# The sign of a 64-bit weight's upper word from GpSimd, one VectorE step fewer per weight block, and every step in a new order

## The chip, the cores and the metric

The kernel runs on one core of a Trainium2 chip. The metric is the device time of one execution in microseconds (us). TensorE (PE, with its weight loads as PEld), VectorE (DVE), ScalarE (ACT), GpSimd (POOL) and the DMA queue of SyncE (SP) each work through their own instructions in order, and semaphores hold an instruction until what it needs is there.

## What is computed

Batch 8, 8 heads, 576 tokens, head size 64, in single precision. Attention keeps only scores within `tau` of the row's maximum; what it gives is the input of a gated MLP that mixes tokens.

```python
scores = scale * np.matmul(q, k.transpose(0, 1, 3, 2))
thresh = np.max(scores, axis=-1, keepdims=True) - tau
scores = np.where(scores >= thresh, scores, -1000000000.0)
attn = softmax(scores)                      # exp, divided by the sum
x = (attn @ v) laid out as (batch, 576, 512)
h = gelu(x @ w_in)                          # 512 -> 1024, tanh form
u, v = h[..., :512], h[..., 512:]
v_n = (v - mean(v)) / sqrt(var(v) + 1e-06) * g_ln
v_s = einsum('ts,bsd->btd', w_sg, v_n) + b_sg
out = x + (u * v_s) @ w_out
```

`w_in` and `w_out` come to the kernel as 64-bit floats, seen as pairs of 32-bit words, and are turned on the chip into a single-precision number and its remainder. `out` is stored transposed.

## The kernel before

A first pass writes down a plan of 4646 steps (`at(kind, key, fn)`, without running them); then `issue` runs them in the sequence of the list `ORDER`, written out by hand as numbers of steps. So `ORDER` sets the order on every engine and queue. `PLACES` gives for each use of PSUM which of the 8 banks it takes.

Attention goes over 32 units `n` of two heads. A unit loads q, k and v, scales q (`q_scale`, L522), copies the last 64 tokens into a tile (`q_tails`, L527), and then goes over five blocks of query tokens: `scores` (L546; L553 for the last block) into two PSUM banks, `maxima` on DVE (L562), `threshold` on POOL (L566), `select` on ACT (L576), `exponentials` on ACT (L582), `turn_blocks` on DVE (L630). The turned blocks go through DRAM and back (`put_blocks`, `get_blocks`), `values` multiplies them by v (L661), `scale_rows` on DVE (L669, L671) divides by the sums, and `x_hi`, `x_lo`, `x_tail` (L676, L679, L682) split the result. Four units make a batch, and `moe(b)` needs all four: products L753, for the first units of batch 0 in two parts (L769, `in_two`), joined on DVE (L779); gelu on ACT and DVE (L725, L738, L740, L732), statistics (L839, L842) on DVE, normalisation on POOL and ACT (L846 to L874), output L961 and a store L964.

The weights are prepared while the first units run. `from_double` runs for 12 blocks of 128x512 numbers (eight of `w_in`, jobs 0 to 7, and four of `w_out`, jobs 14 to 17): `w_load` (L385) brings the words; `magnitude` (L393, ACT) takes the upper word's size times 2^16; `word` step 0 (L398, POOL) bounds it; step 1 (L400, DVE) shifts left by 4 and right by 1, which moves the exponent and leaves the sign bit empty; step 2 (L402, DVE) takes the upper word's sign bit and joins it; step 3 (L404, DVE) keeps sign and exponent; `w_mul` (L413, DVE) multiplies by the lower word; then the high part and the rest, on POOL (L418, L431, L433) or by PE (L424) and ACT (L429). `from_single` does the same for `w_sg` (L460, L461), `tail_weights` (L473, L474) and `bias` for its end. Sixteen `warm` matmuls (L988) of a constant fill gaps on PE.

```python
            elif step == 1:
                engine.tensor_scalar(bits, bits, 4, 1, ALU.logical_shift_left, ALU.logical_shift_right)
            elif step == 2:
                engine.scalar_tensor_tensor(bits, t["up"], 0x80000000, bits, ALU.bitwise_and, ALU.bitwise_xor)
```

Of the kernel before, what the change touches and what calls it, by code (L numbers as in the profile page):

```python
# [12 lines left out]
F32 = mybir.dt.float32  # L13
F32R = mybir.dt.float32r
U32 = mybir.dt.uint32
# [227 lines left out]
def tile_threshold_attention_gated_mlp(  # L243
# [133 lines left out]
    def from_double(src, home, early, put, k):  # L377
# [9 lines left out]
        def magnitude():  # L387
            if early:
                both = cpool.tile([P, 2 * FH], F32, tag=f"z{k % NM}", name=f"wz{k}")
                t["full"], t["pow"] = both[:, 0:FH], both[:, FH:2 * FH]  # L390
            else:
                t["full"], t["pow"] = spares(sp, FH)
# [656 lines left out]
```

## Time and profile before

| | us |
|---|---|
| median of 3 runs | 869.17 (864.87 to 869.45) |
| the profiled execution | 875.15 |
| its span, first to last instruction | 873.3 |
| PE busy | 822.1 (94%) |
| DVE, ACT, POOL busy | 640.5 (73%), 637.8 (73%), 459.9 (53%) |
| granted TensorE clock, mean | 0.978 of full speed |

The profile's page cuts the span into 40 slices. The shares of busy time are means over stages with different limits, so each stage has to be read by itself: the windows view gives busy times by stretch, the waits view who waited for whom, the timeline the instructions in order. A busy PE is not PE at its peak: at half clock the same matmul is busy twice as long.

### The profile page before, as it was taken

Reading aid. Unit: us, or ns where it says so; the run is one execution under the profiler, and the core shown is the slowest. Engines: PE = TensorE matmul, PEld = TensorE weight load, DVE = VectorE, ACT = ScalarE, POOL = GpSimd, SP = SyncE. Lnnn points to the kernel's source line nnn. Section 1 sums busy time; section 2 is a strip of 40 time slices with the busy share of each in tenths; the row PEclk is TensorE's granted clock in tenths of the full one; section 3 lists DMA queues with packets and bytes.
Section 4 is the critical chain, followed back from the end, with each engine's and each line's share of the span. In section 5 each row is a group of like instructions: output and inputs, shape, how many; then the busy total and the mean of one; then the engine's idle time right before and its main releaser. Section 6 shows DMA issues by size and latency. Waiting matters only on the chain.

```text
span 873.3 us, 24720 instructions
## 1 busy us (share of the span) xinstructions
PE 822.1 (94%) x9726; PEld 668.9 (77%) x9726; DVE 640.5 (73%) x1142; ACT 637.8 (73%) x1346; POOL 459.9 (53%) x785
## 2 busy tenths in 40 slices
PE   6788889999999899999999999999999999999998
PEld 3456667876888778887788878887678878887898
DVE  6999798865978477873878848786787838786264
ACT  6868578756988577885779768886697849787271
POOL 3576387443754457443564348534564357535283
PEclk9799999998999999999999999999999999999999
DMA  8897942794676935777356964688466962777401
GB/s 311 205 256 223 259 126 69 208 243 105 180 194 179 222 95 144 199 195 203 109 160 178 230 179 116 168 236 233 131 152 165 250 173 69 183 220 202 108 8 62
DMA packets 218998, 151.74 MB, mean 174 GB/s; under 512 B 32257, under 2 KB 204289, under 8 KB 218882
## 3 DMA queue, kind: packets, MB, share of 16 engines
q1 hardware_dynamic: 218882, 150.16, 64.7%
q8 instruction: 76, 1.25, 0.6%
q14 instruction: 40, 0.33, 0.1%
HBM read 97.68 MB, written 52.43 MB: 172 GB/s over the span
## 4 chain that ended last, share of the span: by engine, by line
PE 53%; DMA 14%; POOL 9%; DVE 8%; ACT 6%; issue 5%; SPq 5%; POOLq 0%; DVEq 0%; ACTq 0%
PE all_banks L753 32%; PE all_banks L546 10%; PE all_banks L661 8%; DMA ir<-ird 4%; DMA pt<-swb 4%; DMA ird<-ir 3%; PE all_banks L553 2%; DVE columns L562 2%; ACT p L576 2%; DMA swb<-pt 2%; SPq L647 2%; ACT p L582 2%; POOL x L679 1%; POOL ot L961 1%; POOL vv L861 1%
## 5 line engine op out<-in xcount | busy, mean ns | idle before, releaser
L576 ACT ACTIVATE p<-all_banks,columns 128x576 f32<-128x576 f32 x288 | 201.7, 737 | 79.2 <-POOL columns L566 78.1
L562 DVE TENSOR_REDUCE columns<-all_banks 128x1 f32<-128x576 f32 x288 | 205.4, 745 | 73.2 <-PE all_banks L546 62.5
L582 ACT ACTIVATE p<-p,columns 128x576 f32<-128x576 f32 x288 | 221.1, 772 | 0.8
L630 DVE STREAM_TRANSPOSE pt<-p 128x576 f32<-128x576 f32 x288 | 208.3, 753 | 16.7 <-ACT p L582 12.1
L546 PE MATMUL all_banks<-rk,rq 64*64 64x288 f32 x2048 | 167.6, 425 | 8.2 <-POOL rq L522 3.3
L661 PE MATMUL all_banks<-pt,rv 64*64 64x128 f32 (+1 forms) x4608 | 156.4, 286 | 14.1 <-DMA pt<-swb 10.7
L661 PEld LDWEIGHTS all_banks<-pt,rv 64*64 64x64 f32 x4608 | 145.1, 134 | 26.0 <-DMA pt<-swb 8.0
L566 POOL TENSOR_TENSOR columns<-columns 128x2 f32<-128x2 f32 (+1 forms) x160 | 35.8, 224 | 207.5 <-DVE columns L562 190.3
L546 PEld LDWEIGHTS all_banks<-rk,rq 64*64 64x64 f32 x2048 | 78.1, 136 | 62.2 <-issue 16.0
L753 PE MATMUL all_banks<-wsh,z 128*128 128x288 f32 (+2 forms) x512 | 116.1, 307 | 2.3 <-ACT p L576 1.9
L753 PE MATMUL all_banks<-wi,x 128*128 128x512 f32 x424 | 113.4, 406 | 5.1 <-ACT p L576 2.5
L753 PE MATMUL all_banks<-x,wi 128*128 128x288 f32 (+2 forms) x720 | 114.9, 301 | 0.1
L753 PEld LDWEIGHTS all_banks<-x,wi 128*128 128x128 f32 x720 | 100.8, 188 | 13.5 <-issue 5.9
L753 PE MATMUL all_banks<-gh,wo 128*128 128x288 f32 (+1 forms) x480 | 107.4, 300 | 0.7 <-DVE ir L671 0.7
L961 POOL TENSOR_TENSOR ot<-ot,x 128x288 f32<-128x288 f32 x112 | 89.9, 808 | 21.6 <-ACT ot L970 19.4
L753 PEld LDWEIGHTS all_banks<-wi,x 128*128 128x128 f32 x424 | 75.9, 189 | 26.8 <-issue 4.0
L753 PEld LDWEIGHTS all_banks<-wsh,z 128*128 128x128 f32 x512 | 85.4, 191 | 14.1 <-issue 5.8
L753 PEld LDWEIGHTS all_banks<-gh,wo 128*128 128x128 f32 x480 | 79.7, 188 | 10.7 <-issue 3.4
L753 PE MATMUL all_banks<-wsl,z 128*128 128x288 f32 (+2 forms) x256 | 74.9, 300 | 0.0
L679 POOL TENSOR_TENSOR x<-ir,x 128x576 fp32r<-128x576 f32 x32 | 45.6, 1425 | 52.8 <-ACT x L676 52.3
L753 PE MATMUL all_banks<-gl,wo 128*128 128x288 f32 (+1 forms) x240 | 70.4, 298 | 0.4 <-POOL gl L936 0.4
L669 DVE TENSOR_TENSOR ir<-all_banks,ir 128x512 f32<-128x512 f32 x32 | 21.9, 684 | 57.3 <-PE all_banks L661 31.8
(161 smaller groups left out, 1147.0 us busy)
## 6 DMA issues: line engine op xcount, KB each, us to landing
rv<-in_vP SPq DMA_DIRECT2D x32, 576.0 KB, 5.3
swb<-pt SPq DMA_DIRECT2D x64, 180.0 KB, 3.7
swb<-pt SPq DMA_DIRECT2D x32, 360.0 KB, 3.9
pt<-swb SPq DMA_DIRECT2D x64, 180.0 KB, 4.7
pt<-swb SPq DMA_DIRECT2D x32, 360.0 KB, 5.3
rq<-in_qT SPq DMA_DIRECT2D x32, 288.0 KB, 4.4
rk<-in_kT SPq DMA_DIRECT2D x32, 288.0 KB, 4.2
swa<-pt SPq DMA_DIRECT2D x32, 288.0 KB, 4.0
```

Of the source, the lines that this page charges most:

```text
L546: nc.tensor.matmul(st["s", h, i][cols, a, 0:HALF], st["q"][rows, i * P + c * D:i * P + (c + 1) * D], st["k"][rows, a * HALF:(a + 1) * HALF ...
L553: nc.tensor.matmul(sc[:, a, 0:HALF], tails[part], st["k"][:, a * HALF:(a + 1) * HALF], start=True, stop=True)
L562: return lambda: nc.vector.tensor_reduce(nm, st["s", h, i][:, :, 0:HALF], AX.XY, ALU.max, negate=True)
L566: return lambda: nc.gpsimd.tensor_tensor(nt, nm, toff[:, 0:1] if i == NM else toff, ALU.subtract)
L576: nc.scalar.activation(halves(st["p", h, i]), st["s", h, i][:, :, 0:HALF], AF.Prelu, bias=columns_of(i)[1][:, h:h + 1], alpha=BIG)
L582: return lambda: nc.scalar.activation(st["p", h, i], st["p", h, i], AF.Exp, bias=toff[:, 0:1], accum_out=l_of[part][:, c:c + 1])
L630: nc.vector.transpose(out, st["p", h, i].rearrange("p (j x) -> p j x", x=BLK))
L661: nc.tensor.matmul(st["acc"][h * D:(h + 1) * D, r, :, c0:c0 + w], v[rows, c, h], x[:, :, h * w:(h + 1) * w], start=(c == 0), stop=(c == PA ...
L669: nc.vector.tensor_tensor(main, acc[:, :, 0:MAINQ], main, ALU.mult)
L679: nc.gpsimd.tensor_tensor(xl_of[b, hp], st["ir"], xh_of[b, hp], ALU.subtract)
L753: nc.tensor.matmul(st["acc"][0:rows[0]] if rows else st["acc"], w, x, start=(j == 0), stop=(j == n - 1))
L961: return lambda: nc.gpsimd.tensor_tensor(o(), o(), x[b, m][:, ts_], ALU.add)
```

## The change

Three things change. The steps of a weight block: step 1 moves from DVE to POOL and becomes the upper word, read as a float, times 0.0 (times 1.0), written to the tile `pow`: zero with the word's sign. Step 2 stays on DVE, now shifts the bounded size left by 3 and joins the sign in the same instruction, from `bits` and `pow`. So a block has three DVE steps instead of four, and two POOL steps of 128x512 instead of one. A function `places` allocates the tiles `full` and `pow` at whichever of the steps comes first, since the sign needs only the loaded words. `ORDER` is new as a whole (4646 steps, the same numbers with the same meanings), and so is `PLACES` (the same 580 uses).

```diff
+        def places():
+            if "full" in t:
+                return
...
         def word(step, engine):
+            places()
             bits = t["full"].bitcast(U32)
...
             elif step == 1:
-                engine.tensor_scalar(bits, bits, 4, 1, ALU.logical_shift_left, ALU.logical_shift_right)
+                engine.tensor_scalar(t["pow"], t["up"].bitcast(F32), 0.0, 1.0, ALU.mult, ALU.mult)
             elif step == 2:
-                engine.scalar_tensor_tensor(bits, t["up"], 0x80000000, bits, ALU.bitwise_and, ALU.bitwise_xor)
+                engine.scalar_tensor_tensor(bits, bits, 3, t["pow"].bitcast(U32), ALU.logical_shift_left, ALU.bitwise_xor)
...
         for step in range(4):
-            if step == 0:
+            if step < 2:
                 put("w_word2", lambda step=step: word(step, nc.gpsimd))
 ORDER = [int(i) for i in """
-    160 16 18 17 162 161 15 19 166 61 168 167 62 169 63 176 177 178 173 170 179 81 164 6 64 238 82 180 65 239 163 192
...
```

Read by kind, the new order keeps the structure: on PE a step stands on average 2.4 places (of 992) from where it stood, on DVE 2.5 (of 1105), on ACT 2.0, on SP 2.3. The largest moves are at the beginning. On PE, nine `warm` steps now stand ahead of the first `scores` and all sixteen within the first 23 places; before, one stood ahead of it and eight came later than place 14. On SP, job 7's load goes out ahead of unit 1's q and k, jobs 1 and 3 go some places later and job 2 some earlier, and unit 2's k goes ahead of the first put. On DVE, 142 steps stood ahead of the fourth unit's `scale_rows` and now 129 do; on POOL the twelve signs stand between place 2 and place 99.

## Rows read from the trace of the kernel before

**Rows 1.** The page: busy tenths in 40 slices of 21.8 us.
```profile
PE   6788889999999899999999999999999999999998
DVE  6999798865978477873878848786787838786264
ACT  6868578756988577885779768886697849787271
POOL 3576387443754457443564348534564357535283
```

**Rows 2.** Windows: length, busy us (instructions) PE, PEld, DVE, ACT, POOL, clock, DMA, GB/s.
```profile
0.00:10.00 10.00, 5.12 (x34) 2.29 (x34) 2.68 (x10) 2.20 (x3) 2.89 (x14) 1.00 0.78 246
10.00:60.00 50.00, 41.67 (x374) 23.68 (x374) 48.13 (x80) 41.69 (x85) 28.57 (x48) 0.86 0.91 262
60.00:120.00 60.00, 51.15 (x672) 37.48 (x670) 53.80 (x85) 42.91 (x89) 34.68 (x54) 0.97 0.83 220
120.00:160.00 40.00, 37.11 (x387) 29.90 (x388) 33.75 (x67) 32.80 (x73) 29.92 (x42) 0.91 0.40 104
160.00:840.00 680.00, 657.51 (x8045) 546.44 (x8045) 486.59 (x871) 507.89 (x1077) 345.36 (x607) 0.99 0.66 172
```

**Rows 3.** Waits in 0 to 160 us: total us, times, longest.
```profile
POOL columns L566 <- DVE columns L562: 32.5, 22, 3.9
ACT p L576 <- POOL columns L566: 19.4, 16, 2.7
PE all_banks L769 <- DVE vv L732: 3.9, 1, 3.9
POOL wt L473 <- DMA wt9h<-in_w_sgT: 2.9, 1, 2.9
```

**Rows 4.** Instructions of lines L400, L402: ns min/median/max, first and last start, shapes.
```profile
L400 DVE TENSOR_SCALAR wz<-wz x4: 416/572/1484, 33.0 to 58.2; 128x512 uint32<-128x512 uint32 x4
L400 DVE TENSOR_SCALAR wt<-wt x3: 416/418/1491, 30.4 to 114.4; 128x512 uint32<-128x512 uint32 x3
L400 DVE TENSOR_SCALAR wt1h<-wt1h x1: 418/418/418, 11.0 to 11.0; 128x512 uint32<-128x512 uint32 x1
...
L402 DVE SCALAR_TENSOR_TENSOR wz<-raw_wi,wz x4: 629/672/712, 36.7 to 69.1; 128x512 uint32<-128x512 uint32 x4
```

**Rows 5.** Groups by line in 0 to 125 us: busy us, mean ns, idle before.
```profile
L400 DVE TENSOR_SCALAR wz<-wz 128x512 uint32<-128x512 uint32 x4 | 3.0, 761 | 0.0
L400 DVE TENSOR_SCALAR wt<-wt 128x512 uint32<-128x512 uint32 x3 | 2.3, 775 | 0.0
L398 POOL TENSOR_SCALAR wt<-wt 128x512 f32<-128x512 f32 x3 | 1.8, 613 | 0.6 <-ACT wt L393 0.4
L431 POOL TENSOR_TENSOR wt3h<-wt3h,wt3l 128x512 f32<-128x512 f32 x1 | 1.3, 1282 | 0.0
```

**Rows 6.** Timeline of DVE and POOL near 114 us: start, us, instruction.
```profile
114.34 1.29 POOL L861 TENSOR_TENSOR vv<-vv,g_bc 128x512 f32<-128x512 f32 x1
...
114.42 1.49 DVE L400 TENSOR_SCALAR wt<-wt 128x512 uint32<-128x512 uint32 x1
...
117.10 1.77 DVE L402 SCALAR_TENSOR_TENSOR wt<-raw_wo,wt 128x512 uint32<-128x512 uint32 x1
118.80 1.48 DVE L404 TENSOR_SCALAR wt12l<-wt12h 128x512 uint32<-128x512 uint32 x1
120.20 0.67 DVE L732 SCALAR_TENSOR_TENSOR vv<-gt,all_banks 128x512 f32<-128x512 f32 x1
```

**Rows 7.** Timeline of the beginning.
```profile
1.20 1.22 PE L988 MATMUL all_banks<-warm 128*128 128x256 f32 x2 [1.20 <-DVE warm L985]
...
5.75 3.89 PE L546 MATMUL all_banks<-rk,rq 64*64 64x288 f32 x32 [3.32 <-POOL rq L522]
...
8.01 1.42 DVE L562 TENSOR_REDUCE columns<-all_banks 128x1 f32<-128x576 f32 x2 [2.85 <-PE all_banks L546]
...
11.17 1.20 PE L546 MATMUL all_banks<-rk,rq 64*64 64x288 f32 x16
...
16.22 1.89 PE L988 MATMUL all_banks<-warm 128*128 128x256 f32 x8
```

**Rows 8.** Timeline: the fourth unit's scale_rows.
```profile
103.26 0.69 DVE L669 TENSOR_TENSOR ir<-all_banks,ir 128x512 f32<-128x512 f32 x1 [2.46 <-PE all_banks L661]
```

**Rows 9.** Waits of PE in 160 to 874 us.
```profile
PE all_banks L661 <- DMA pt<-swb: 8.6, 9, 2.0
PE all_banks L753 <- ACT p L576: 4.4, 2, 2.5
```

More of the change, by code (lines that the diff above doesn't have):

```diff
@@ L31 @@
 ORDER = [int(i) for i in """
[194 rows of a table removed]
[194 rows of a table added]
 """.split()]
 PLACES = "".join("""
-    0204600245462010104620042604546202466042601642260426004232306426046254602567016240452604167242164261024674217024
-    6402640740624076420724670234606401642643164302643264064536040246754204270642014270246704204237640640670420376403
-    2406041742064230461346024604264206724104261462146024216246245216720540274520164042674023064206452602060256450246
-    2402610246704240237041643246032451606214264206742124160246421426702462064023640760400246024572052046502720427014
-    2640234067340646201426102640126240167214242601224760234567207240624042701246024674202640462306420654016752023516
-    47075236017013254304
+    0101010102046002446023246045440264204634026406206240642602462024606245026546723530652605467052062046520672074205
+    6402562062016420264602345640262067205402602754025042062360530654320620642560230652064520602675204052026046720564
+    0256720340642016245621062506202645062306542062605423062606201465264106250162340246072401264162450626020467240762
+    0470264072340604672034602540623670450246202650126420564206205206742602464023674064040246204572042601642364064560
+    2304670423074062401640216420641264516206720562340625012673403460246046301642146234604623046306242605672301212374
+    65301624705215342070
 """.split())
@@ L385, in load @@
             nc.sync.dma_start(t["raw"], src.bitcast(U32))
-        def magnitude():
+        def places():
+            if "full" in t:
+                return
             if early:
@@ L392, in magnitude @@
                 t["full"], t["pow"] = spares(sp, FH)
+        def magnitude():
+            places()
             nc.scalar.activation(t["full"], t["up"].bitcast(F32), AF.Abs, scale=UPPER_MORE)
         def word(step, engine):
+            places()
             bits = t["full"].bitcast(U32)
```

387 rows, old and new, of the table ORDER are left out of this document.

## The prediction

> **What bounds the kernel now.** I read the 40 slices of the page first [rows 1]. PE stands at 9 in nearly all slices behind the seventh, so from about 150 us on the kernel is held by PE. In the first seven it is not: there DVE is the row that stays near 9. The windows by stage say the same in microseconds [rows 2]. From 10 to 120 us DVE is busy 48.13 + 53.80 = 101.9 of 110 us (93%); PE 92.8 of 110, and part of that at half pace, since the granted clock is 0.86 in the first half; ACT 84.6; POOL 63.3. From 160 to 840 us PE is busy 657.5 of 680 us (97%) and DVE 72%. So a microsecond of DVE is worth most of a microsecond before about 140 us and nothing behind it, where PE is the limit and the other engines wait for it.
>
> What makes DVE full at the beginning is that the first attention units and the 12 weight blocks run together. The waits of that stretch follow the same line [rows 3]: POOL waits for the maxima of DVE (32.5 us in total), ACT for POOL's thresholds, which stand behind those maxima (19.4 us), and PE for ACT to free PSUM. The clearest place is 114 to 121 us [rows 6]: three weight instructions of DVE take 1.49, 1.77 and 1.48 us, the second half of a gelu (L732) stands behind them until 120.20 us, and PE waits 3.9 us for it [rows 3]. All 12 instructions that the change takes from DVE start between 11.0 and 114.4 us [rows 4], that is, inside this stretch.
>
> **What leaves DVE.** Step 1 (L400): 12 instructions. Four are 3.0 us together, three 2.3, and five single ones 0.42 each (0.39 to 0.43), 2.1 [rows 4, 5]: 7.4 us. An undisturbed one takes 0.42 us, so 12 of them would be 5.0; the other 2.4 are waits inside the instruction, as in the one of 1.49 us that starts 0.08 us behind a POOL instruction (L861) of 1.29 us [rows 6]. Step 2 remains one instruction with two tensors of 128x512 from SBUF, and one of its kind takes 0.63 to 0.71 us [rows 4]; nothing is added for it. The chain of one block also gets a step shorter, but a block isn't waited for by itself as long as DVE is full. With DVE busy 93% of the stretch, 0.93 x 7.4 = 6.9 us of it should come off the stretch. The ends are 7.4 (all of it) and 0 (another engine takes over at once). Read in the order: the fourth unit's scale_rows, which is at 103.26 us [rows 8] and without which batch 0's gated MLP can't go on, has 129 DVE steps ahead of it instead of 142; 11 of the 13 are these. So the new order does use the place.
>
> **What POOL gets.** 12 signs of 128x512. The nearest row is L398, also one tensor and two scalars of that shape: 0.61 us [rows 5], in all 7.4 us. What no row shows is POOL reading every second word; the upper bound is the POOL instruction that reads two tensors, 1.28 us [rows 5], in all 15.4 us. I take 0.61, the same operation and the same number of elements. [...] POOL is idle 110 - 63.3 = 46.7 us of the stretch [rows 2], which covers either price on the whole. It doesn't cover it in place: behind a sign in POOL's queue stand thresholds, and ACT's select waits for those. 7.4 us in 110 put a sign in the way of a threshold once in 15, for 0.3 us on average; 22 waits for thresholds' maxima are recorded in the stretch [rows 3], so perhaps 25 thresholds, and 25 / 15 x 0.3 = 0.5 us. With 1.28 us a sign it is four times that, 2.0; the lower end is 0.
>
> **What the two do to each other.** The row of 1.49 us shows that a POOL instruction holds up a DVE instruction of a weight block. The same can happen to the remaining three steps, 36 instructions in the stretch. In 12 such instructions it cost 2.4 us while POOL was busy 63.3 us; POOL gets 7.4 us more, 12%; so 3 x 2.4 x 0.12 = 0.9 us. The ends are 0 and twice that, 1.8 (the dearer sign). [...]
>
> **What the new order moves at the beginning.** DVE's first maximum is at 8.01 us [rows 7], behind a first pair of score products (0 to 16 of the 32 records that go at the pace of the lower TensorE level, 16 in 1.95 us; at 11.17 us 16 take 1.20). Nine warm matmuls now stand ahead of it, starting at 1.20 us. At the pace of the row at 16.22 us one takes 1.89 / 4 = 0.47 us, at half pace 0.94. All at full pace, they end at 5.4 us, ahead of the score operands (5.75), and the first scores run fast: the maximum comes 1.95 - 1.20 = 0.75 us earlier. All at half pace, they end at 9.7, and the maximum follows at about 9.7 + 1.20 + 0.3 = 11.2 us, 3.2 us later, or 3.9 if the scores too are slow. No row shows which; between the ends I take the middle of the warm end, 7.5 us, with fast scores behind it: 9.0 us, 1.0 us later. DVE is empty until then, so all of it is on the path. The warm matmuls taken from 15 to 80 us filled gaps in which PE waited; they cost and give nothing except clock, and the clock there fell anyway (0.86). The weight loads that change places on SP and unit 2's earlier k I cost at nothing: the waits of this stretch name a load only once, 2.9 us for a block (L473) that the order hardly moves [rows 3].
>
> **What it moves later.** Behind 160 us the steps stand two or three places from where they stood, and no stage changes place. PE's waits there sum to 22.5 us in 680 [rows 2], mostly short ones for blocks on their way through DRAM (8.6 us in 9 waits) and for PSUM (4.4 us in 2) [rows 9]. A new order draws these anew: zero on balance, 4 us either way. The lead of the beginning is kept, since PE is full from there and has the same work left.
>
> **The sum.** -6.9 + 0.5 + 0.9 + 1.0 = -4.5 us. The profiled execution took 875.15 us (span 873.3 and 1.85 around it), so it would become 870.6. The three runs have their median 6.0 us lower, with the same program; the lead is one of work, not of a share, so I take it from the median as it is: 869.2 - 4.5 = 864.7 us. That is 0.52%; about 0.5% (4.3 us) is what a measurement of this kernel can tell from no change, so the forecast stands on that edge.
>
> **The rivals.** (a) The place is taken over: DVE becomes free, but the beginning is then held by thresholds and select, by the half clock of PE, or by blocks on their way through DRAM. For it: ACT is busy 84.6 of the 110 us and PE 92.8 [rows 2], and both wait in a ring with DVE. Against it: ACT's waits end with POOL, and POOL's with DVE's maxima [rows 3]. A fused step as dear as both old ones (1.07 us) would end here too. The gain is then 0 to 2 us: 868 us. (b) More than the removed time: the 3.9 us wait of PE at 117 us sits behind three such DVE instructions [rows 3, 6]; when they go or move, PE fills earlier, keeps its higher clock, and some of the 22.5 us behind goes too. 6.9 + 3.9 with 1 or 2 us of costs: 860 us. Against it: part of the 3.9 is the same time as the 6.9. (c) Slower: a sign needs its weight's load only, and the order sets it early in POOL's queue, two of the 12 within the first eight places. POOL waits there until the load is in, and thresholds, tails and scales behind it wait too, and with them ACT, PSUM and PE. The wait of 2.9 us for a load at L473 [rows 3] is the size of one. It decides when such waits on the path exceed 4.5 us, two of them, and at 0.5% slower, 8.8 us, three of them: 3 x 2.9 - 4.5 = 4.2, 874 us with the dearer sign's extra 1 us. Against it: only one such wait is in the present stretch, and the two at the front wait for a load that the first magnitude needs as well.
>
> **How the numbers follow.** Forecast (862 to 867.5): 0.47, a little over half of it beyond 0.5%. Taken over (a): 0.22. More (b): 0.19. Slower (c): 0.12. Faster by over 0.5%: 0.26 + 0.19 = 0.45. Within: 0.21 + 0.22 = 0.43. Slower: 0.12. The range from 857 to 873 takes in the forecast with its bounds (worst start +2.9, dearer sign +2.4, a worse later order +4; or best start -1.8, later order -4) and most of (a) to (c).
>
> **What would show it.** Right: L400's new form with 12 instructions on POOL at about 0.61 us, the join on DVE at 0.65 to 0.7; the first maximum near 9 us; the fourth unit's scale_rows near 98.5 us; DVE still above 90% from 10 to 115 us; no PE wait of 3.9 us behind L732; from 160 us on the same 97%. Wrong: scale_rows of the fourth unit at 103 us or later, with ACT or POOL full instead of DVE (a); at 95 or earlier (b); POOL waits for weight loads of several us ahead of the sign (c); or a lead at 140 us that is gone at 840.

## The result, and the profile after

The changed kernel takes 859.7 us (median of 11 runs, 851.5 to 864.8) beside 869.1 us for the kernel before in the same runs: a ratio of 0.988, 95% interval 0.985 to 0.992. It is faster by 1.2%, some 10 us, more than twice the 4.5 us of the forecast and inside its range. The profiled execution took 859.30 us, near its median; that of before lay 6 us over its own (875.15), so a difference of the two traces shows 16 us where 10 are to be explained. Single executions of one kernel scatter with a standard deviation of about 3 us (those of before in these runs go from 864.4 to 874.6), so below a sum is taken from medians and ratios, and a trace says where. A ratio is the measured one with its interval and not the quotient of the two medians, from which it differs by up to 0.3%.

The busy tenths of the page and the windows by stage of the kernel after answer to [rows 1, 2] (columns as there):

```profile
PE   7787898999999899999999999999999989999998
DVE  5998699776869477885878658884887738786255
```

```profile
0.00:10.00 10.00, 8.04 (x50) 5.74 (x50) 2.65 (x10) 1.98 (x2) 3.59 (x15) 1.00 0.76 233
10.00:60.00 50.00, 39.29 (x469) 22.53 (x473) 45.79 (x72) 43.47 (x89) 33.63 (x55) 0.97 0.95 276
60.00:120.00 60.00, 52.74 (x571) 35.84 (x564) 48.30 (x82) 41.70 (x85) 35.20 (x57) 0.91 0.77 196
160.00:840.00 680.00, 664.91 (x8148) 556.88 (x8147) 490.56 (x883) 515.15 (x1095) 358.54 (x622) 1.00 0.65 172
```

From 10 to 120 us DVE's busy time fell from 101.9 to 94.1 us (86% of the stretch), as the sum wanted, and the waits of POOL and ACT for its maxima with it (32.5 and 19.4 us in [rows 3], 23.6 and 12.3 now). But PE isn't fuller there: 92.0 of 110 us against 92.8, at a mean clock of 0.94 against 0.92. PE gained behind 160 us, where the forecast wanted nothing: 664.9 of 680 us instead of 657.5, at a clock of 1.00 instead of 0.99. And the fourth unit's scale_rows, which DVE's relief was to move from 103.26 us [rows 8] to about 98.5, starts at 102.83. The timeline shows what it waits for now (first number the start):

```profile
90.34 0.20 DVE L601 STREAM_TRANSPOSE ir<-l 128x32 f32<-128x32 f32 x1
...
90.57 0.33 SPq L606 DMA_DIRECT2D ird<-ir  x1
...
96.92 0.62 SPq L611 DMA_DIRECT2D ir<-ird  x1
...
99.25 1.27 SPq L618 DMA_DIRECT2D ir<-ird  x2
...
102.83 0.69 DVE L675 TENSOR_TENSOR ir<-all_banks,ir 128x512 f32<-128x512 f32 x1 [2.33 <-DMA ir<-ird]
```

The reciprocals of the unit go out to DRAM at 90.57 us and come back by reads that are issued from 96.92 on; DVE is idle for 2.33 us until they are in. Before, the same step waited 2.46 us for PE. DVE had idle time right ahead of the step in both, so less DVE work at this place could not move it; whether less DVE work further ahead could is what run d1 below asks.

The new steps, by line (ns min/median/max, first and last start; L406 is the sign, L408 the join):

```profile
L406 POOL TENSOR_SCALAR wz<-raw_wi x4: 650/764/977, 23.1 to 50.8; 128x512 f32<-128x512 f32 x4
L406 POOL TENSOR_SCALAR wt3l<-raw_wi x1: 1217/1217/1217, 12.3 to 12.3; 128x512 f32<-128x512 f32 x1
...
L408 DVE SCALAR_TENSOR_TENSOR wt<-wt x3: 648/674/684, 33.2 to 124.5; 128x512 uint32<-128x512 uint32 x3
L408 DVE SCALAR_TENSOR_TENSOR wt1h<-wt1h,wt1l x1: 692/692/692, 12.3 to 12.3; 128x512 uint32<-128x512 uint32 x1
```

### The profile page after: what moved, and what is told of

Read it like the earlier page. It is cut to its first block, busy times and chain, and to the rows that moved or that the text cites. A ratio compares the mean times of both kernels' runs of the same rounds, so it can differ in the third digit from the quotient of the medians.

```text
span 857.5 us, 24743 instructions
## 1 busy us (share of the span) xinstructions
PE 815.6 (95%) x9726; PEld 663.8 (77%) x9726; DVE 632.2 (74%) x1130; ACT 638.5 (74%) x1346; POOL 467.2 (54%) x797
## 4 chain that ended last, share of the span: by engine, by line
PE 58%; DMA 14%; DVE 8%; POOL 6%; SPq 5%; issue 4%; ACT 4%; DVEq 0%; POOLq 0%; ACTq 0%
PE all_banks L759 34%; PE all_banks L552 11%; PE all_banks L667 9%; DMA pt<-swb 5%; DMA ir<-ird 3%; PE all_banks L559 3%; DVE columns L568 3%; DVE pt L636 2%; SPq L653 2%; DMA swb<-pt 2%; SPq L646 2%; DMA ird<-ir 1%; ACT p L582 1%; ACT p L588 1%; DMA out_T<-ot 1%
## 5 line engine op out<-in xcount | busy, mean ns | idle before, releaser
L759 PE MATMUL all_banks<-wsh,z 128*128 128x288 f32 (+2 forms) x512 | 114.2, 303 | 2.1 <-DVE uu L738 1.5
L759 PE MATMUL all_banks<-wi,x 128*128 128x512 f32 (+1 forms) x424 | 112.9, 402 | 0.9 <-POOL x L685 0.8
L967 POOL TENSOR_TENSOR ot<-ot,x 128x288 f32<-128x288 f32 x112 | 89.6, 804 | 22.5 <-ACT ot L976 17.7
L759 PEld LDWEIGHTS all_banks<-wi,x 128*128 128x128 f32 (+1 forms) x424 | 74.5, 185 | 22.9 <-issue 4.4
L682 ACT ACTIVATE x<-ir 128x576 fp32r<-128x576 f32 x32 | 21.8, 682 | 50.3 <-DVE ir L677 45.6
```

The lines of the kernel that those rows point to most:

```text
L682: nc.scalar.activation(xh_of[b, hp], st["ir"], AF.Copy)
L759: nc.tensor.matmul(st["acc"][0:rows[0]] if rows else st["acc"], w, x, start=(j == 0), stop=(j == n - 1))
L967: return lambda: nc.gpsimd.tensor_tensor(o(), o(), x[b, m][:, ts_], ALU.add)
```

## The experiments

Three things changed: the arithmetic of a block, the order of the first 160 us, and the order behind it. Wherever a cut fits (no PSUM bank in use on both sides by different places), a kernel can take one order up to there and the other from there on. "Old" is the kernel before, "new" the changed one; "rest" is all that stands behind about 160 us. At each cut the banks of `PLACES` go along with the steps that use them, and 471 of its 580 entries differ between the two kernels. So "order" below means sequence and banks together, and no run tells the two apart. All times are medians, with the ratio to the kernel before and its 95% interval. Line numbers shift by a few from kernel to kernel with the length of the list.

### Arithmetic and order taken apart

The new order with the old arithmetic (a1):

```diff
-                engine.tensor_scalar(t["pow"], t["up"].bitcast(F32), 0.0, 1.0, ALU.mult, ALU.mult)
+                engine.tensor_scalar(bits, bits, 4, 1, ALU.logical_shift_left, ALU.logical_shift_right)
...
-                engine.scalar_tensor_tensor(bits, bits, 3, t["pow"].bitcast(U32), ALU.logical_shift_left, ALU.bitwise_xor)
+                engine.scalar_tensor_tensor(bits, t["up"], 0x80000000, bits, ALU.bitwise_and, ALU.bitwise_xor)
...
-            if step < 2:
+            if step == 0:
```

> The new order of all steps with the old arithmetic: the word is shifted right in a VectorE instruction of its own (12 of about 0.42 us undisturbed), directly ahead of the join in the new order; no sign on GpSimd. Theory S (the steps, as the prediction's sum has it): the new order alone gives back the 6.9 us of VectorE time, so the time lies at 866 to 869, a ratio to before of 0.996 to 1.000. Theory O (the order): VectorE's relief is not what ends the beginning, and the gain comes from where the steps stand; the time stays at 859 to 861, ratio 0.988 to 0.991.

Measured: 861.5 us, 0.9929 (0.9895 to 0.9963). Some 6 of the 10 us (3.2 to 9.1) are there without the arithmetic, where theory S allows 3.5 at most. The old order with the new arithmetic (a2) has the same lines the other way round:

> The old order with the new arithmetic: sign as a product with zero on GpSimd directly behind the clip of the same block, shift and sign joined in one VectorE instruction; every other step stands where it stood. Theory S: 7.4 us less VectorE work in the first 120 us shows without the new order as well, 863 to 866, ratio 0.993 to 0.997. Theory O: the fourth unit's scale_rows stays at 103 us and the time stays at 868 to 870, ratio 0.999 to 1.002. Third case (GpSimd's queue): a sign placed ahead of thresholds that an order written for other costs wants early makes it slower, 871 to 874.

Measured: 866.2 us, 0.9972 (0.9939 to 1.0005). So the arithmetic is worth about 2.4 us here, with an interval from 5.3 us to nothing, in which most of theory S's range still lies; what speaks against S is a1, and a4 below. Next, the two halves of the order, cut at about 160 us:

```diff
 ORDER (a3, new arithmetic; a4 the mirror image with the old arithmetic)
-steps among the first 826 of the old order: in the old order
+steps among the first 826 of the old order: in the new order
 all later steps: in the old order
```

> The new arithmetic, with the steps that the old order has among its first 826 (up to about 160 us, all 12 weight blocks among them) in the new order, and all later steps as the old order has them. Theory B (the beginning gives the lead, as the prediction says): 860 to 862, ratio 0.989 to 0.992. Theory L (the traces' scale_rows are level up to 135 us and part only behind 170 us, so the lead comes from the later order): 867 to 869, ratio 0.997 to 1.000.

Measured: 866.7 us, 0.9963 (0.9934 to 0.9992): no better than the arithmetic in the old order (866.2).

> The old arithmetic, with the first 834 steps of the new order (up to about 160 us) as the old order has them, and all later steps in the new order. Theory B: nothing of the lead, 867 to 869, ratio 0.997 to 1.000. Theory L: nearly the whole lead without any of the change in the weight blocks, 860 to 862, ratio 0.989 to 0.992.

Measured: 861.0 us, 0.9902 (0.9867 to 0.9937). Nothing of the weight blocks is changed in this kernel and nothing ahead of 160 us, and it has nearly the whole lead. Theory L holds, theory B falls. The combination that was missing (e3), the new arithmetic and the new rest with the old start:

> New arithmetic, the first 834 steps of the new order (to about 160 us) in the old order with each sign directly behind its clip, warm matmuls and loads where they were; all later steps in the new order. If the three parts add (arithmetic -2.5, rest -7.8, the new start 0): 858 to 860, the same as the changed kernel. If the new start is worth what the prediction's sum says (DVE's time only used by the new order): 863 to 865.

Measured: 861.0 us, 0.9912 (0.9884 to 0.9940), between the two forecasts. With these five and the kernels before and after, each part has three pairs (differences of the ratios, times 869 us): the order behind 160 us gives -8.5 (a4 to before), -7.0 (after to a3) and -5.2 us (e3 to a2), mean -6.9; the arithmetic -2.4, -4.1 and +0.9, mean -1.9; the new start -0.8, +2.3 and -2.6, mean -0.4. A pair is uncertain by 3 to 4 us and a mean of three by about 2, and the pairs share kernels. The rest is clear of that, the start isn't, and the arithmetic lies on the edge.

### Where the later order gains

In the three traces that have the old rest unchanged behind old or new starts (before, a2, a3) PE stands still and then runs slowly at the same two places. (Three more runs with the old rest, d1 to d3 below, wait there too, up to 5 us earlier or later, d1 at the first place for only 1.0 us.) The windows show it (length, PE busy, clock, DMA), first for a3, then for the kernel after:

```profile
190.00:202.00 12.00, 9.08 (x48) 0.86 0.94 245
328.00:340.00 12.00, 10.07 (x67) 0.86 0.75 194
...
334.00:336.00 2.00, 2.00 (x7) 0.54 0.96 286
```

```profile
190.00:202.00 12.00, 11.08 (x155) 1.00 0.89 232
328.00:340.00 12.00, 11.85 (x154) 1.00 0.54 130
```

Length less busy time times clock is what PE lost: 4.2 and 3.3 us with the old rest, 0.9 and 0.2 with the new. The second place in a3's timeline:

```profile
330.30 0.76 DVE L585 TENSOR_REDUCE columns<-all_banks 128x1 f32<-128x576 f32 x1
...
330.81 0.30 PE L776 MATMUL all_banks<-wsh,z 128*128 128x288 f32 x1
...
330.94 0.30 PE L776 MATMUL all_banks<-wsl,z 128*128 128x288 f32 x1
...
331.02 0.68 DVE L761 SCALAR_TENSOR_TENSOR gt<-gt,vv 64x512 f32<-64x512 f32 x1
...
331.63 0.74 DVE L585 TENSOR_REDUCE columns<-all_banks 128x1 f32<-128x576 f32 x1
...
332.45 0.69 POOL L589 TENSOR_TENSOR columns<-columns 128x2 f32<-128x2 f32 x1 [1.32 <-DVE columns L585]
...
333.18 1.37 ACT L599 ACTIVATE p<-all_banks,columns 128x576 f32<-128x576 f32 x2 [0.81 <-POOL columns L589]
...
333.97 0.45 PE L776 MATMUL all_banks<-wsh,z 128*128 128x288 f32 x1 [1.93 <-ACT p L599]
334.22 0.44 PE L776 MATMUL all_banks<-wsl,z 128*128 128x288 f32 x1
```

The order has one instruction of the gelu (L761) between the two maxima of a block; the thresholds wait for the second, the select for the thresholds, and a product of the gated MLP on PE for the PSUM bank that the select reads: 1.93 us. Behind the wait a product takes 0.44 us, where one takes 0.30 ahead of it; they overlap, and from one start to the next it is 0.25 us instead of 0.13. The granted clock is 0.54 from 334 to 336 us, behind 1.00 from 328 to 334. Of the 3.3 us lost here 1.9 are the wait and 1.4 the slow stretch behind it. The slow stretch doesn't always follow: in d3's trace the same wait of 1.9 us stands at a clock of 1.00, and 1.9 us are lost in all. The kernel before has the same wait; it is one of the two for L576 in [rows 9]. So 13 steps were moved by hand in the kernel before (b1), with nothing else changed:

```diff
 ORDER
-xh(5) ... xt(5) ... xl(5) ... idt(6) ... irw(6) ... put(7,*) irr(6,0) irt(6,0) irr(6,1) irt(6,1)
+xh(5) xl(5) ... xt(5) ... idt(6) ... irw(6) ... irr(6,0) irt(6,0) irr(6,1) put(7,*) irt(6,1)
...
-madd(v4) ... pe(u0,2) pe(u0,2) ... s(13,1) nm stt1(v4) nm ... thr tanh(v4) ... sel sel
+s(13,1) pe(u0,2) ... nm nm madd(v4) ... thr ... sel sel vn(v3) ... tanh(v4)
```

> The kernel before, old arithmetic, with 13 steps moved by hand at two places: around 177 to 187 us the low half of unit 5's x ahead of its tail, unit 6's idt, irw and three of its four reads of the inverse earlier (the chain that ends in the scale_rows at 193.85 us); around 327 to 333 us the scores (13,1), their two maxima, threshold and selects ahead of the work of the gated MLP that they stand behind (the PE wait of 1.9 us for a select). Everything else as before. Theory P (the lead of the later order is two or three single places where PE stood still for about 2 us and then ran at the lower clock): PE's lost time at 190 to 202 and at 330 to 340 us, 3 to 4.5 us each in the old order, falls below 1 us each, and the time to 862 to 865, ratio 0.992 to 0.996. Theory Q (the later order helps all along, by many small things): the two places close, or new ones open behind them, and the time stays at 867 to 870, ratio 0.998 to 1.001.

Measured: 869.9 us, 1.0032 (1.0002 to 1.0063): no gain. Its trace says why for the second place (windows, and the waits of PE from 325 to 345 us):

```profile
190.00:202.00 12.00, 11.04 (x136) 1.00 0.92 247
326.00:344.00 18.00, 15.10 (x134) 1.00 0.64 164
```

```profile
PE all_banks L770 <- POOL zt L893: 1.3, 1, 1.3
PE all_banks L770 <- DVE uu L749: 1.0, 1, 1.0
PE all_banks L563 <- ACT p L593: 0.6, 1, 0.6
```

The wait for the select is gone, and PE loses 2.9 us in 326 to 344 us instead, waiting for the gated MLP's own steps (uu, zt), which stand behind what was moved ahead of them. The first place did close (1.0 us lost in 190 to 202). Still the time didn't fall, so theory P falls in this form; about 3 us less were lost at the first place, and where they went the run doesn't show. Two more cuts ask where along the order the lead lies:

```diff
 ORDER, old arithmetic
-old order throughout
+e1: old to about 160 us, new to about 347 us, old to the end
+e2: old to about 290 us, new to the end
```

> The kernel before, old arithmetic, in its own order up to about 160 us and again behind about 347 us; only the steps between are in the new order. Theory M (the lead of the later order lies where the traces' PE time parts, 160 to 347 us: 18.1, 12.7 and 12.3 us lost there and up to 440 us in three kernels with the old rest, 6.2, 5.3 and 4.2 in three with the new): 862 to 864, ratio 0.992 to 0.995. Theory Q (many small things along the whole order): 865 to 867, ratio 0.996 to 0.998. Theory N (a stall that goes comes back as another one, as when the steps were moved by hand): 868 to 870.

Measured: 869.5 us, 1.0009 (0.9979 to 1.0038). Theory M falls, although both places are closed in its trace:

```profile
190.00:202.00 12.00, 12.00 (x112) 1.00 0.87 243
328.00:340.00 12.00, 12.00 (x91) 1.00 0.43 114
```

> The counterpart of the middle alone: the kernel before, old arithmetic, in its own order for the first 1556 steps (to about 290 us, the tenth unit's scale_rows) and from there in the new order. Theory V (the lead is made mostly behind 290 us: scale_rows of the profiles with the new rest gain 8.5 us on average from the tenth unit to the last, those with the old rest 3.9, and the tail behind the last is 1.0 us shorter): 862.5 to 865, ratio 0.993 to 0.996, with PE idle and slow at 190 to 202 us as before and not at 330 to 340. Theory N (only the whole later order holds a lead, a part of it gives it back): 867 to 870, ratio 0.998 to 1.001. Theory M (the part to 290 us has most of it): 866 to 868.

Measured: 860.6 us, 0.9913 (0.9882 to 0.9943): the steps behind 290 us give a lead as large as a4's (0.9902), within an uncertainty of 4 us. Its trace has the first place open and the second closed:

```profile
190.00:202.00 12.00, 9.35 (x48) 0.86 0.93 236
328.00:340.00 12.00, 12.00 (x91) 1.00 0.49 124
```

(Its profiled execution, 866.2 us, is one of two of its six that lie 5 us over the others; PE waits 3.0 us for DVE near 605 us in it.) To compare traces whose orders differ, marks are needed that have the same work ahead of them. Units 2, 7, 16 and 24 are such, numbered from 0 as in the code (so the fourth unit is number 3, and what the expectation above calls the tenth is number 10): PE has the same steps ahead of their scale_rows in both orders. Times between their starts in the traces, the end being the execution's time (d1, d2, d3 and c1 are the runs of the next section, which change only the beginning):

| | rest | 2 to 7 | 7 to 16 | 16 to 24 | 24 to the end |
|---|---|---|---|---|---|
| before | old | 124.2 | 244.2 | 199.4 | 222.0 |
| a2 | old | 119.7 | 241.2 | 199.5 | 221.3 |
| a3 | old | 121.2 | 241.0 | 198.3 | 222.0 |
| b1, by hand | old | 121.3 | 241.9 | 197.1 | 223.2 |
| d1 | old | 117.7 | 239.5 | 197.7 | 221.1 |
| d2 | old | 123.4 | 240.8 | 197.8 | 223.3 |
| d3 | old | 122.7 | 239.1 | 202.6 | 225.8 |
| e1 | new 160 to 347 us | 122.0 | 238.9 | 200.0 | 222.8 |
| e2 | new from 290 us | 122.2 | 237.4 | 201.3 | 219.6 |
| a1 | new | 118.6 | 237.2 | 198.9 | 221.1 |
| a4 | new | 120.0 | 235.4 | 197.6 | 218.9 |
| e3 | new | 119.6 | 237.4 | 197.6 | 219.0 |
| after | new | 118.7 | 236.4 | 197.9 | 221.0 |
| c1 | new | 120.5 | 235.6 | 201.0 | 221.4 |

Between units 7 and 16 (about 206 to 445 us) the seven with the old order take 239.1 to 244.2 us, the six with the new one (e2 from 290 us on) 235.4 to 237.4: 4.5 us by the means, and the ranges don't meet. From unit 24 to the end the means are 222.7 for the eight with the old ending and 220.2 for the six with the new one, 2.5 us, but here the ranges overlap by 0.3 us. Together 7.0, as much as the pairs gave for the later order (6.9) and near e2's lead of 7.6. Between units 2 and 7 the five with the new order from 160 us on take 2.1 us less by the mean than the eight with the old one there, inside the spread of those.

What PE waited for says the same. Between units 7 and 16 PE loses (idle time, and busy time times what the granted clock lacks of 1.00) 5.8 to 12.3 us in the seven and 2.4 to 4.8 in the six. In six of the seven, all but b1, 1.9 us of it are the one wait for a select at the second place above, which none of the other six has. Behind unit 24 PE waits for a load of v in all eight traces with the old ending, 0.8 to 2.9 us in sum (a3's line below: total, times, longest), and in none of the six with the new one:

```profile
PE all_banks L684 <- DMA rv<-in_vP: 1.8, 2, 1.0
```

Which of these waits the new order removes by a move of steps, which by other banks, and which only by the shift of everything ahead of them isn't shown. The table shows e1 faster by 2.2 us between 7 and 16 and by nothing elsewhere, and its time is that of before. b1 lies among the others with the old order, apart from 0.6 us between 16 and 24.

### The price of an engine's time in the beginning

The kernel before without its shifts (d1):

```diff
             elif step == 1:
-                engine.tensor_scalar(bits, bits, 4, 1, ALU.logical_shift_left, ALU.logical_shift_right)
+                pass
```

> The kernel before without its 12 right shifts on VectorE (the words of the weights then stay shifted, which is left out of the computation); nothing is put on GpSimd and no step moves. The price of VectorE's time in the beginning by itself. Theory S (VectorE is the bound there, as the prediction says): 6.9 us less, 861 to 863, ratio 0.991 to 0.994, and the fourth unit's scale_rows 5 us earlier. Theory R (the beginning is held by a ring of all engines and the transfers, VectorE only a part of it): 1 to 3 us less, 866 to 868, ratio 0.9965 to 0.999, scale_rows of the fourth unit at 102 to 103 us.

Measured: 865.5 us, 0.9967 (0.9938 to 0.9997), 2.9 us less (0.3 to 5.4) for the 7.4 us taken away: theory R rather than S, whose 6.9 us lie outside. In its trace the fourth unit's scale_rows doesn't move and waits for PE as before:

```profile
103.31 0.69 DVE L669 TENSOR_TENSOR ir<-all_banks,ir 128x512 f32<-128x512 f32 x1 [2.44 <-PE all_banks L661]
```

More work for DVE instead, a mask behind each shift (d2):

```diff
                 engine.tensor_scalar(bits, bits, 4, 1, ALU.logical_shift_left, ALU.logical_shift_right)
+                engine.tensor_scalar(bits, bits, 0x7FFFFFFF, 0x7FFFFFFF, ALU.bitwise_and, ALU.bitwise_and)
```

> The kernel before with a second VectorE instruction of the same shape behind each of the 12 shifts (a mask that changes nothing), 12 x 0.42 to 0.62 us = 5 to 7.4 us more on VectorE between 11 and 115 us. Theory S: 5 to 7 us slower, 874 to 876, ratio 1.006 to 1.008. Theory R: 1 to 3 us slower, 870 to 872, ratio 1.001 to 1.0035.

Measured: 872.7 us, 1.0052 (1.0022 to 1.0083), 4.5 us more (1.9 to 7.2). The groups by line show what was added (busy us, mean ns), 5.9 us in all with five single ones:

```profile
L401 DVE TENSOR_SCALAR wz<-wz 128x512 uint32<-128x512 uint32 x4 | 2.0, 499 | 0.1
L401 DVE TENSOR_SCALAR wt<-wt 128x512 uint32<-128x512 uint32 x3 | 1.3, 428 | 0.1
```

So a microsecond more on DVE costs 0.8 us and one less gives back 0.4, by the middle of intervals that overlap (0.3 to 1.2 and 0.0 to 0.7): between the two theories, and whether the price differs by direction isn't shown. Then more for the transfers (d3, on the kernel before):

```diff
             nc.sync.dma_start(t["raw"], src.bitcast(U32))
+            again = dpool.tile([P, FH], F32, tag="again", name=f"again{k}").bitcast(U32)
+            nc.sync.dma_start(again, src.bitcast(U32)[:, 0:FH])
```

> The kernel before with half of each of the 12 weight blocks (256 KB) sent a second time, from DRAM to DRAM, right behind its load: 3.1 MB more for the DMA queues in the first 110 us (they are at a share of 0.86 there, 239 GB/s) and 12 more issues on the queue of SyncE. Theory D (the transfers hold the beginning): the blocks on their way through DRAM land later and the time rises by 5 us and more, 874 to 880, ratio over 1.006. Theory R: 1 to 3 us, 870 to 872. Theory S: under 1 us, 869 to 870, since VectorE's work doesn't change.

Measured: 869.7 us, 1.0041 (1.0010 to 1.0072), 1 to 6 us more (too wide to tell theory D from R), while the share of the DMA queues from 10 to 120 us rose from 0.86 to 0.93:

```profile
10.00:120.00 110.00, 92.22 (x1044) 58.69 (x1044) 100.50 (x162) 83.17 (x171) 61.85 (x101) 0.97 0.93 269
```

And more for GpSimd (c1, on the changed kernel):

```diff
                 engine.tensor_scalar(t["pow"], t["up"].bitcast(F32), 0.0, 1.0, ALU.mult, ALU.mult)
+                engine.tensor_scalar(t["pow"], t["up"].bitcast(F32), 0.0, 1.0, ALU.mult, ALU.mult)
```

> The changed kernel with each of the 12 signs on GpSimd made twice, 12 x 0.65 = 7.8 us more on GpSimd between 8 and 115 us. By the prediction's terms (a threshold delayed, 0.5, and VectorE held up, 0.9): 861 to 862.5. If GpSimd's queue is the bound of the beginning: 865 to 868. If GpSimd's time there is free: 859 to 860.5.

Measured: 863.2 us, 0.9915 (0.9884 to 0.9947), against 0.9882 of the changed kernel: 2.9 us more, with an uncertainty of 4. It can't tell the prediction's terms from the others, but GpSimd's queue as the bound (865 to 868) it makes unlikely. No run shows one engine that holds the beginning alone: a microsecond of DVE is worth a part of one (0.4 and 0.8 us in d1 and d2), more transfers cost some time too (1 to 6 us in d3), and a price for POOL's time isn't shown.

## Why the prediction was right, and where it was not

The direction and the range held; the sum did not, and that the time still fell into the range was luck. -6.9 + 0.5 + 0.9 + 1.0 is -4.5; measured is -10, of which the term that the sum set at zero has 7.

- *DVE's relief, -6.9.* Mis-sized. The 7.4 us did go, but a stretch in which DVE is busy 93% isn't one in which each microsecond of it is worth 0.93. Taken away by itself it gave 2.9 us (0.3 to 5.4, d1). The step that failed reads the fourth unit's scale_rows by the number of DVE steps ahead of it. The row of that step [rows 8] had 2.46 us of idle DVE in front, waiting for PE: what was late there was another chain, and it showed ahead of time. The forecast's own signs failed: scale_rows came at 102.83 us instead of about 98.5, and DVE was busy 85% from 10 to 115 us (89.5 of 105 us) instead of above 90%. Rival (a)'s sign of 103 us or later was missed by 0.2 us, and no full ACT or POOL took the place of DVE (81.5 and 64.0 of the same 105 us).
- *Signs on POOL, +0.5, and mutual hold-ups, +0.9.* The signs take 0.65 to 1.22 us, 9.2 us in all instead of 7.4. In the times the two terms can't be seen singly: the arithmetic in the old order (a2, -2.4) and the shifts merely left out (d1, -2.9) differ by 0.5 us, less than either interval. In the traces the hold-ups can be sized where the order is the same: the 36 DVE steps left in the blocks take 29.2 us in before and 30.4 in a2, 28.5 in a1 and 28.4 in after, and 30.3 in c1 with 24 signs. A dozen signs thus cost DVE -0.1 to 1.9 us, and the 0.9 lies between. The traces have either side as the one held up: the sign of 1.22 us starts at 12.32 us, 0.04 behind a join of 0.69 us, and in [rows 6] it was the DVE step that came second, 0.08 us behind, and took 1.49 us where an undisturbed one takes 0.42. What no row of before showed, POOL reading every second word, costs little in the trace: 0.65 to 0.68 us undisturbed beside 0.61 for the clip.
- *The start, +1.0.* DVE's first maximum came at 8.32 us, 0.3 later than before [rows 7], not 1.0. The nine warm matmuls and the scores in the trace:

```profile
1.20 5.93 PE L994 MATMUL all_banks<-warm 128*128 128x256 f32 x18 [1.20 <-DVE warm L991]
7.07 2.17 PE L552 MATMUL all_banks<-rk,rq 64*64 64x288 f32 x32
...
8.32 2.75 DVE L568 TENSOR_REDUCE columns<-all_banks 128x1 f32<-128x576 f32 x4 [2.62 <-PE all_banks L552]
```

  They end at 7.1 us, near the 7.5 assumed, which was a middle taken between two ends, and the scores behind them run fast, 32 records in 2.17 us instead of 3.89. The windows show a granted clock of 1.00 from 0 to 10 us for both, so the slow scores of before weren't at a lower granted clock. The rest of the new start is worth nothing that three pairs could show.
- *The later order, 0 with 4 either way.* This is the step that failed most. It read the right rows [rows 9], the two waits for a select with 4.4 us among them, and then let a new order "draw them anew". The new order has neither of these two, and PE's waits behind 160 us are mainly those for blocks through DRAM:

```profile
PE all_banks L667 <- DMA pt<-swb: 8.6, 12, 1.6
PE all_banks L759 <- DVE ir L677: 2.0, 1, 2.0
PE all_banks L552 <- ACT p L582: 1.3, 3, 0.9
```

  What the sum could have had from before's rows: such a wait can cost more than its length, when PE runs at a lower granted clock behind it (0.50 over 2 us in before and a2, 0.54 in a3, where 3.3 us were lost for a wait of 1.9; 1.00 in d3, where 1.9 were), and the steps at these places do differ in the two lists. That closing these two places alone gives nothing (b1), nor the new order from 160 to 347 us (e1), could not be read there.
- *The rivals.* (a) was right on the beginning, and 868 was what it would have given alone; (b) named the size (860) and "some of the 22.5 us behind" as a source, but by way of the wait at 117 us. That wait is gone in the kernel after (its longest of PE up to 160 us is 2.4 us), yet a4 and e2, with the old beginning, still have it at its full 3.9 us and have the lead as well, so it isn't the cause. (c) did not come: POOL waits for a weight's load ahead of a sign once, 1.9 us up to 8.42 us. Its premise that the waits name a load only once misses one at the front: ACT waits 6.3 us for the first block's load, up to 8.34 us in before, and 6.3 us in after too.

So the time lies in the range mainly for a reason that the sum didn't contain; the forecast of faster stood on a term worth a third of what it was given.

## What to carry to other kernels

An engine that is busy 93% of a stretch need not be its bound: look at the step that ends the stretch and what ended the idle time ahead of it, and price a microsecond by a run before it is counted, since here it gave 0.4 when taken away (0.0 to 0.7), not 0.93. Where the change carries a new order of everything, the order is the change: cut it at places where both orders agree on what is in use, run the halves crosswise, and compare at marks with the same work ahead. A wait that is cured by hand in a full order can come back at the work that was passed over, as b1's second place did.

## What the hardware showed beyond that

A PE wait of 1.9 us cost 3.3 us in a3's trace: products followed each other by 0.25 us behind it instead of 0.13, at a granted clock of 0.54, though a single one took 0.44 us instead of 0.30. In d3's trace the same wait cost its 1.9 us alone, at a clock of 1.00. A sign on GpSimd, 0.65 us undisturbed, takes up to 1.22 beside other work, and a dozen signs add -0.1 to 1.9 us to the DVE steps of the same blocks. And the same kernel's executions scatter with a standard deviation of about 3 us without any change in its order, so one trace, like the one of 875.15 us, can carry 6 us that aren't the kernel's.
